# First token group of an mLSTM cell with a SwiGLU block: output gates loaded ahead of the weights, later loads in another order and other buffers, some gate work moved to VectorE

## The chip, the cores and the metric

The kernel runs on one core of one Trainium2 chip. The metric is the device time of one execution in microseconds. A core has a matrix engine (TensorE, PE in the profile; its weight loads are PEld), a vector engine (VectorE, DVE), a scalar engine (ScalarE, ACT), a general engine (GpSimd, POOL) and a sync engine (SyncE, SP), which here only issues transfers. Each engine works through its own instructions in order. Transfers between the main memory and the on-chip memory are issued from SP's queue and from ACT's queue (SPq and ACTq in the profile) and are carried out by 16 DMA engines. An instruction of ACT that stands behind a transfer's issue in ACT's program waits until that issue is through.

## The reference

Two stages follow each other. The first is a recurrent cell over 4 batches, 8 heads, 768 positions and 40 features (cut to what matters):

```python
for t in range(S):
    m_new = maximum(f_gate[t] + m, i_gate[t])
    C = exp(f_gate[t] + m - m_new) * C + exp(i_gate[t] - m_new) * outer(v[t], k[t])
    n = exp(f_gate[t] + m - m_new) * n + exp(i_gate[t] - m_new) * k[t]
    y[t] = sigmoid(o_gate[t]) * (C @ q[t]) / maximum(abs(n @ q[t]), 1)
```

The second is a feed-forward block over the 3072 tokens, with x the cell's output of 320 features per token: `(silu(x @ w_gate) * (x @ w_val)) @ w_out`, with 1536 hidden features. The cell's inputs are float32. The three weight matrices arrive as float64: 7.9 MB for the gate and value weights together and 3.9 MB for the output weights.

## The kernel before

**Groups.** The 768 positions are cut into 6 groups of 128. In each group the cell is computed in its parallel form: a matrix of weights per head made of running sums and running maxima of the gates, multiplied with the products of queries and keys, plus the contribution of the state carried over from earlier groups. Then 512 tokens (4 batches times 128 positions) go through the feed-forward block. The first group is special: its gates are handled by `first_*` functions, and while its feed-forward block runs, the weights are still being loaded and converted. Groups 2 to 6 use `gated` (L886) and `project_seven` (L794) with weights that are already in place; nothing in them is touched by the change.

**Weights.** `piece_load(p)` (L165) loads piece p of the weights as raw 64-bit words. Pieces 0 and 1 are one 128-column block of the gate and value weights each, pieces 2 to 6 are two blocks each, pieces 7 to 9 are the output weights. A piece of gate and value weights comes as three transfers: the gate half (64 partitions) on SP's queue, and the value half in two parts (the other 64 partitions) on ACT's queue. A piece of two blocks has 640 KB of gate weights and 512 KB plus 128 KB of value weights. The raw words land in a rotating buffer `raw` of two places, or in a "home", a stretch of a tile that is not used yet (`h_sb`, `wo_sb`).

**Conversion.** Block j becomes float32 in three steps: `scale(j)` (L216) on ACT (two instructions, L221 and L223), `join(j)` (L226) on DVE (L230 and L231), and `rounded(j)` (L235) on POOL or DVE (L238). The tile `top` between the first two steps has one buffer, so `scale` of the next block waits for `join` of this one.

**The first feed-forward block.** `hidden(0, m)` (L737) for m = 0 to 11 does ten matmuls on PE (20 records in the trace, L745) with block m, then the conversions that the table `ahead` names for m, then the SiLU on ACT (L750) and the product on DVE (L751). There are two pairs of result banks, so the matmuls of m wait for the product of m - 2; the banks are shared with the state of the first group, which ACT copies out at L142 (`first_kept`). After each m the functions in `slots[m]` follow. They prepare the second group: running sums of the later gates (`late_sums`, L315), their running maxima (`late_maxima`, L320), which are stored to main memory as `M_dram` (L1002 of `slots[1]`) and read back spread over the partitions into `w_sb` (`weights_load`, L501), the decay factors (`late_decay`, L325; an exponential on ACT in `slots[2]`; `decay_rows`, L719; `decay`, L727), transposes on PE that need that exponential (`late_turns`, L712), and transposes of keys and queries (`turn`, L343). `weights_sub` (L506), `weights_mask` (L510) and `weights_exp` (L531) make the second group's weights of `w_sb`. For the later groups a table `cap` (L516) and `weights_cap` (L523) do the masking instead.

**Order.** Each engine runs its instructions in the order in which the program names them; nothing reorders them. A further rule comes from how the program is built: eight semaphores tell of landings, they are dealt to the transfers in turn, and the issue of a transfer waits until the previous transfer with the same semaphore has landed. That earlier transfer can belong to the other queue. The built program names each such wait.

Of the kernel before, what the change touches and what calls it, by code (L numbers as in the profile page):

```python
# [13 lines left out]
AF = mybir.ActivationFunctionType  # L14
# [5 lines left out]
SUB = 64  # L20
# [4 lines left out]
def kernel(  # L25
# [139 lines left out]
    def piece_load(p, home=None, parts=(0, 1, 2)):  # L165
        kind, m, n = PIECES[p]
        if kind == "gv":
# [4 lines left out]
            queues = (nc.sync,) + 2 * (nc.scalar,)  # L172
# [12 lines left out]
        if p < 2 and not homes:  # L185
            for x in (1, 0):
                homes[x] = conv.tile([128, 4 * NKC * 128], U32, name="raw")
        if p in homes:
            raw = homes[p]
        elif home is None:  # L190
            raw = conv.tile([128, 4 * NKC * 128], U32, name="raw")
        else:
            raw = home.rearrange("p a t -> p (a t)").bitcast(U32)
# [121 lines left out]
    def late_sums():  # L315
        nc.vector.tensor_tensor_scan(flat(f_sb), flat(keep1), flat(f_sb), 0.0, op0=ALU.mult, op1=ALU.add)
        nc.gpsimd.memset(step1, 0.0)
        nc.gpsimd.tensor_sub(i_sb, i_sb, f_sb)
# [191 lines left out]
    def weights_mask(P):  # L510
        for i in range(2):
            w = w_sb[half(i), heads(P)]
            nc.gpsimd.affine_select(w, w, compare_op=ALU.is_ge, fill=NEG, base=0, pattern=[[0, UH], [1, SUB]],
                                    channel_multiplier=-1)

# [137 lines left out]
    piece_load(0)  # L653
# [19 lines left out]
    first_scores(1)  # L673
    scale(0)
    piece_load(1)
    sig(0)
    fill("y", 4, True)
    first_own(2)
    first_x(2)
    first_gate(0, (G, G), G)  # L680
    fill("y", 3, True)
    first_own(3)
    fill("y", 6, False)
    sig(1)
    piece_load(2, h_sb[:, 1:1 + NKC], (0, 1))
    late_gates()
    first_x(3)
    seam(0, 0, (A, A, A, A))
    first_gate(1, (V, V), A)
    ps0 = first_state(0, "gen")  # L690
# [5 lines left out]
    piece_load(2, parts=(2,))  # L696
    scale(1)
    piece_load(3)
# [6 lines left out]
    late_sums()  # L705
# [292 lines left out]
    def load_all(dst, a, n):  # L998
# [9 lines left out]
    ahead.update({4: [6], 5: [7, 8], 6: [9], 7: [10], 8: [11], 9: [], 10: [], 11: []})  # L1008
    slots = {
        0: [run(load_all, k_sb, k, 1), run(piece_load, 4, wo_sb), run(load_all, q_sb, q, 1)],  # L1010
        1: [run(late_maxima), run(nc.sync.dma_start, out=M_dram, in_=flat(M_sb)), run(late_decay)],
        2: [run(piece_load, 5, h_sb[:, NH - NKC:]), run(nc.scalar.activation, step1, step1, AF.Exp), run(decay_rows)],
        3: [run(late_turns)],
        4: [run(piece_load, 6), run(decay), run(cap_table), run(weights_load, 1), run(load_all, v_sb, v, 1)],
        5: [run(turn, 0, (A, A), (A, V))],
        6: [run(turn, 1, (A, A), (A, V)), run(piece_load, 7)],
# [129 lines left out]
```

## Time and profile before

| what | us |
|---|---|
| median of 3 runs | 522.8 (519.88 to 525.58) |
| the profiled execution | 526.02 |
| its span, first to last instruction | 524.2 |
| PE busy in the span | 506.9 (97%) |
| DVE, POOL, ACT busy | 334.6, 259.1, 206.8 |

The profile is of one execution. Times in it count from the start of the span. The busy shares are means over stages with different limits: PE is the bound from about 60 us to the end, while the first 60 us, where the weights arrive, have waits. So the first stage has to be read by itself: in the chain of waits (the work that ended last, followed back), in the timelines of single engines, where a bracket gives the idle time before a row and what ended it, and in tables by stretch of time, whose last three columns are the granted clock of PE, the busy share of the DMA engines and the rate that they moved.

### The profile page before, as it was taken

To read this page: it belongs to the slowest core of one execution; us is meant where nothing else is said; L and a number is where in the kernel's file an instruction comes from. 1 tells how busy PE (TensorE), PEld (TensorE's weight loads), DVE (VectorE), ACT (ScalarE), POOL (GpSimd) and SP (SyncE) were. 2 spreads that over 40 slices of the span, in tenths; PEclk is the share of its full clock that TensorE was granted. 3 is DMA by queue.
4 is the path that set the end of the run, shared out by engine and by line. 5 is a ranking of instruction groups with operands and counts; after the bars stand their busy time and mean duration, and the time that the engine had idled before them with its cause. 6 is when DMAs were issued, how large, how long until landed. Compare 5 with 4: busy or idle time off the path is not lost.

```text
span 524.2 us, 15080 instructions
## 1 busy us (share of the span) xinstructions
PE 506.9 (97%) x6446; PEld 425.6 (81%) x6446; DVE 334.6 (64%) x541; ACT 206.8 (39%) x400; POOL 259.1 (49%) x278
## 2 busy tenths in 40 slices
PE   9988499999999999999999999999999999999997
PEld 3843254676788999988899998899988899988897
DVE  5759358688878858867656867656847655233421
ACT  3552555447652227623137523137522231133210
POOL 3304134746777782455761455761455760166720
PEclk9999699999999999999999999999999999999999
DMA  9999998689830897230996230797100200100001
GB/s 144 186 202 142 188 193 234 96 171 124 143 38 3 128 136 84 56 38 6 139 132 74 54 39 5 136 130 78 41 1 10 43 5 14 39 1 0 1 14 39
DMA packets 205499, 43.31 MB, mean 83 GB/s; under 512 B 193432, under 2 KB 200600, under 8 KB 205432
## 3 DMA queue, kind: packets, MB, share of 16 engines
q1 hardware_dynamic: 202836, 38.34, 47.6%
q10 hardware_dynamic: 2596, 4.00, 4.0%
q8 instruction: 51, 0.84, 0.7%
q14 instruction: 16, 0.13, 0.1%
HBM read 35.68 MB, written 4.01 MB: 76 GB/s over the span
## 4 chain that ended last, share of the span: by engine, by line
PE 89%; DMA 6%; SPq 4%; issue 1%; ACT 0%; ACTq 0%; DVE 0%; DVEq 0%
PE gv_x L893 25%; PE o_ps L816 22%; PE gv_y L893 20%; PE gv_ps L745 8%; PE o_ps L762 5%; DMA o_sb<-in_o_gate_dram 2%; PE inter L422 2%; PE sp L373 2%; PE intra L431 2%; SPq L196 2%; DMA h_sb<-in_moe_w_val_dram 2%; DMA q_sb<-in_q_dram 2%; PE add L399 1%; SPq L248 1%; SPq L138 1%
## 5 line engine op out<-in xcount | busy, mean ns | idle before, releaser
L893 PE MATMUL gv_x<-xT,wgv_sb 64*128 64x256 f32 x720 | 89.7, 377 | 0.0
L893 PEld LDWEIGHTS gv_x<-xT,wgv_sb 64*128 64x128 f32 x720 | 70.0, 187 | 7.9 <-issue 0.2
L816 PE MATMUL o_ps<-wo_sb,h_sb 128*128 128x160 f32 x480 | 67.4, 300 | 0.0
L816 PEld LDWEIGHTS o_ps<-wo_sb,h_sb 128*128 128x128 f32 x480 | 65.6, 190 | 1.7 <-issue 1.7
L745 PE MATMUL gv_ps<-xT,wgv_sb 64*128 64x512 f32 x240 | 59.0, 625 | 2.6 <-ACT top L221 1.2
L941 ACT ACTIVATE h_sb<-gv_x 128x256 f32<-128x256 f32 x30 | 11.5, 384 | 118.0 <-PE gv_x L893 118.0
L745 PEld LDWEIGHTS gv_ps<-xT,wgv_sb 64*128 64x128 f32 x240 | 24.9, 196 | 30.8 <-issue 24.7
L893 PE MATMUL gv_y<-xT,wgv_sb 64*128 64x256 f32 x360 | 44.2, 376 | 0.0
L893 PE MATMUL gv_y<-q_sb,wgv_sb 64*128 64x256 f32 x360 | 44.2, 376 | 0.0
L893 PEld LDWEIGHTS gv_y<-q_sb,wgv_sb 64*128 64x128 f32 x360 | 35.2, 187 | 3.9
L893 PEld LDWEIGHTS gv_y<-xT,wgv_sb 64*128 64x128 f32 x360 | 35.2, 187 | 3.9
L384 POOL TENSOR_TENSOR vw_sb<-v_sb,w_sb 128x656 f32<-128x656 f32 x10 | 14.9, 1490 | 40.7 <-ACT w_sb L529 40.6
L816 PE MATMUL o_ps<-wT,S 128*128 128x160 f32 x240 | 33.4, 299 | 0.0
L816 PEld LDWEIGHTS o_ps<-wT,S 128*128 128x128 f32 x240 | 32.9, 190 | 0.0
L893 PE MATMUL gv_x<-q_sb,sw 64*128 64x256 f32 x240 | 31.2, 376 | 0.0
L529 ACT ACTIVATE w_sb<-w_sb,g_T 128x64 f32<-128x64 f32 x128 | 31.0, 333 | 0.0
L914 POOL TENSOR_TENSOR h_sb<-tmp 128x512 f32<-128x512 f32 x13 | 16.5, 1269 | 24.0 <-ACT tmp L913 24.0
L914 POOL TENSOR_TENSOR h_sb<-x_sb 128x512 f32<-128x512 f32 x12 | 15.8, 1313 | 24.6 <-ACT x_sb L913 24.6
L893 PE MATMUL gv_y<-q_sb,sw 64*128 64x256 f32 x200 | 27.5, 389 | 0.3 <-issue 0.3
L934 POOL TENSOR_TENSOR tmp<-tmp 128x512 f32<-128x512 f32 x15 | 20.0, 1330 | 15.7 <-DVE tmp L933 15.7
L783 POOL TENSOR_TENSOR S<-h_sb 128x256 f32<-128x256 f32 x30 | 22.6, 753 | 9.2 <-DVE h_sb L914 7.3
L933 DVE TENSOR_TENSOR tmp<-tmp,gv_y 128x1024 f32<-128x1024 f32 x15 | 18.1, 1205 | 14.2 <-PE gv_y L893 12.5
(228 smaller groups left out, 993.2 us busy)
## 6 DMA issues: line engine op xcount, KB each, us to landing
w_sb<-M_dram SPq DMA_DIRECT2D x10, 512.0 KB, 7.0
v_sb<-in_v_dram SPq DMA_DIRECT2D x12, 320.0 KB, 5.9
o_sb<-in_o_gate_dram SPq DMA_DIRECT2D x12, 320.0 KB, 4.4
raw<-in_moe_w_out_dram SPq DMA_DIRECT2D x3, 1280.0 KB, 6.2
k_sb<-in_k_dram SPq DMA_DIRECT2D x10, 320.0 KB, 7.5
x_sq<-k_sb SPq DMA_DIRECT2D x64, 40.0 KB, 2.0
q_sb<-in_q_dram SPq DMA_DIRECT2D x32, 64.0 KB, 3.2
out_dram<-tmp SPq DMA_DIRECT2D x24, 80.0 KB, 1.7
```

The source lines that it names most:

```text
L196: queue.dma_start(out=raw[r].rearrange("p (a d) -> p a d", a=a)[:, cs], in_=w.bitcast(U32))
L384: eng.tensor_tensor(vw_sb[:, heads(P)], v_sb[:, heads(P)], w_sb[:, heads(P), last].to_broadcast([128, UH, D1]), op=ALU.mult)
L529: nc.scalar.activation(w_sb[:, h], w_sb[:, h], AF.Exp, bias=g_T[:, n, h:h + 1], scale=-1.0)
L745: nc.tensor.matmul(ps[i], lhsT=wgv_sb[half(i), m, kc, :], rhs=x[half(i), kc, :], start=(kc == 0), stop=(kc == NKC - 1))
L762: nc.tensor.matmul(ps[u], lhsT=hid(g, m)[:, ts(u, L)], rhs=wo_sb[:, m, :], start=(m == 0), stop=(m == NFC - 1))
L783: eng.tensor_tensor(S1[:, k], lo[:, second_half], hi[:, second_half], op=ALU.add)
L816: nc.tensor.matmul(node[x][:, i], lhsT=lhs(k)[:, ts(i, L)], rhs=rhs(k), start=start and k == 0 and i == 0, stop=stop and k == KH - 1, skip ...
L893: nc.tensor.matmul(ps[:, i, cols], lhsT=lhs(c)[half(i)], rhs=rhs(c)[half(i)], start=start and c == 0, stop=stop and c == n - 1, skip_group ...
L914: (nc.vector if k == KH - 1 else nc.gpsimd).tensor_tensor(h_sb[:, 2 * k + 1], uw[:, 0], uw[:, 1], op=ALU.mult)
L933: nc.vector.tensor_tensor(uw, uw, y, op=ALU.add)
L934: nc.gpsimd.tensor_tensor(uw[:, :, second_half], uw[:, :, second_half], uw[:, :, first_half], op=ALU.add)
L941: nc.scalar.activation(h[:, first_half], x[:, 0, first_half], AF.Silu)
```

## The change

- In the first group the output gates (`o_sb`) are loaded directly behind q, k and v; piece 0 follows them and piece 1 comes at once after piece 0. The value halves of both are issued from ACT after the copies of the first group's transposes. Both sigmoids (`sig`) stand ahead of the second set of scores, and `scale(0)` after the first gating.
- Piece 2 is loaded in one call. Piece 3 goes into the end of `h_sb`, piece 4 into the buffer that piece 1 leaves (`homes[4] = homes[1]`), piece 5 into `wo_sb`, piece 6 into `raw`. Piece 4 is now called before the second group's keys.
- From piece 5 on, all three transfers of a piece are on SP's queue.
- `late_sums` moves into `slots[1]`, `late_maxima` and the store of `M_dram` into `slots[2]`, `late_decay` and its exponential into `slots[3]`, `decay_rows`, `late_turns` and the cap table into `slots[4]`, `decay` into `slots[7]`. `weights_load`, pieces 5 and 6 and the values of the second group follow the store of `M_dram` in `slots[2]`, all on SP.
- The subtraction in `late_sums` is on VectorE. The mask of the second group is a maximum with the cap table on VectorE (`weights_cap`, in `slots[6]`) instead of four selections on GpSimd.
- `ahead` converts one block in each of m = 5 to 9 instead of two in m = 5 and one in m = 6 to 8.

```diff
--- before.py
+++ after.py
@@ -169,7 +169,7 @@
             gate_w, val_w = (w[:, m * 128:(m + n) * 128].rearrange("(c p) f -> p c f", p=HP) for w in (moe_w_gate, moe_w_val))
             src = [(slice(0, HP), slice(0, NKC), gate_w), (slice(HP, 128), slice(0, NKC - 1), val_w[:, 1:]),
                    (slice(HP, 128), slice(NKC - 1, NKC), val_w[:, 0:1])]
-            queues = (nc.sync,) + 2 * (nc.scalar,)
+            queues = (nc.sync,) + 2 * (nc.scalar if p < 5 else nc.sync,)
         else:
             a, d = n, DM
             src = [(slice(0, 128), slice(0, n), moe_w_out[m * 128:(m + n) * 128].rearrange("(a p) d -> p a d", p=128))]
@@ -183,8 +183,9 @@
                         nc.sync.dma_start(out=wgv_sb[r, m + x, cs], in_=w[:, :, ts(x, 128)])
             return
         if p < 2 and not homes:
-            for x in (1, 0):
+            for x in (0, 1):
                 homes[x] = conv.tile([128, 4 * NKC * 128], U32, name="raw")
+            homes[4] = homes[1]
         if p in homes:
             raw = homes[p]
         elif home is None:
@@ -315,7 +316,7 @@
     def late_sums():
         nc.vector.tensor_tensor_scan(flat(f_sb), flat(keep1), flat(f_sb), 0.0, op0=ALU.mult, op1=ALU.add)
         nc.gpsimd.memset(step1, 0.0)
-        nc.gpsimd.tensor_sub(i_sb, i_sb, f_sb)
+        nc.vector.tensor_sub(i_sb, i_sb, f_sb)
 
     def late_maxima():
         nc.vector.tensor_copy(step1[:, 0:1, 0:1], f0[0:BH, end].unsqueeze(1))
@@ -507,12 +508,6 @@
         gb = g_T[:, n, heads(P)].unsqueeze(2).to_broadcast([128, UH, SUB])
         nc.vector.tensor_tensor(w_sb[:, heads(P)], gb, w_sb[:, heads(P)], op=ALU.subtract)
 
-    def weights_mask(P):
-        for i in range(2):
-            w = w_sb[half(i), heads(P)]
-            nc.gpsimd.affine_select(w, w, compare_op=ALU.is_ge, fill=NEG, base=0, pattern=[[0, UH], [1, SUB]],
-                                    channel_multiplier=-1)
-
     def cap_table():
         nc.gpsimd.memset(cap, -3e38)
         for i in range(2):
@@ -650,7 +645,6 @@
     for x in range(B):
         first_inputs(1, x)
     turn_one(0, k_sb, kT, (V, A))
-    piece_load(0)
     load(o_sb, o_gate, 0, 0)
     load(o_sb, o_gate, 0, 1)
     for x in range(B):
@@ -670,39 +664,40 @@
     first_own(1)
     first_x(0)
     first_x(1)
-    first_scores(1)
-    scale(0)
+    piece_load(0)
     piece_load(1)
     sig(0)
+    sig(1)
+    first_scores(1)
     fill("y", 4, True)
     first_own(2)
+    piece_load(2, h_sb[:, 1:1 + NKC])
+    late_gates()
     first_x(2)
     first_gate(0, (G, G), G)
+    scale(0)
     fill("y", 3, True)
     first_own(3)
+    first_x(3)
     fill("y", 6, False)
-    sig(1)
-    piece_load(2, h_sb[:, 1:1 + NKC], (0, 1))
-    late_gates()
-    first_x(3)
     seam(0, 0, (A, A, A, A))
     first_gate(1, (V, V), A)
+    piece_load(3, h_sb[:, NH - NKC:], (0,))
     ps0 = first_state(0, "gen")
     ps1 = first_state(1, "gen")
     join(0)
     rounded(0, V)
     seam(0, 1, (A, V, V, A))
     fill("add", 14, False)
-    piece_load(2, parts=(2,))
+    piece_load(3, parts=(1, 2))
     scale(1)
-    piece_load(3)
+    piece_load(4)
     first_kept(0, ps0, V)
     join(1)
     first_kept(1, ps1, A)
     rounded(1, V)
     nc.scalar.activation(warm, warm, AF.Silu)
     convert(2, V)
-    late_sums()
 
 
     pair = early.tile([BH, PP], F32)
@@ -1005,16 +1000,17 @@
     on_vector = (9, 10, 11)
     ahead = {m: [m + 2] for m in range(4)}
     ahead[0] = []
-    ahead.update({4: [6], 5: [7, 8], 6: [9], 7: [10], 8: [11], 9: [], 10: [], 11: []})
+    ahead.update({4: [6], 5: [7], 6: [8], 7: [9], 8: [10], 9: [11], 10: [], 11: []})
     slots = {
-        0: [run(load_all, k_sb, k, 1), run(piece_load, 4, wo_sb), run(load_all, q_sb, q, 1)],
-        1: [run(late_maxima), run(nc.sync.dma_start, out=M_dram, in_=flat(M_sb)), run(late_decay)],
-        2: [run(piece_load, 5, h_sb[:, NH - NKC:]), run(nc.scalar.activation, step1, step1, AF.Exp), run(decay_rows)],
-        3: [run(late_turns)],
-        4: [run(piece_load, 6), run(decay), run(cap_table), run(weights_load, 1), run(load_all, v_sb, v, 1)],
+        0: [run(load_all, k_sb, k, 1), run(load_all, q_sb, q, 1)],
+        1: [run(late_sums)],
+        2: [run(late_maxima), run(nc.sync.dma_start, out=M_dram, in_=flat(M_sb)), run(weights_load, 1),
+            run(piece_load, 5, wo_sb), run(piece_load, 6), run(load_all, v_sb, v, 1)],
+        3: [run(late_decay), run(nc.scalar.activation, step1, step1, AF.Exp)],
+        4: [run(decay_rows), run(late_turns), run(cap_table)],
         5: [run(turn, 0, (A, A), (A, V))],
-        6: [run(turn, 1, (A, A), (A, V)), run(piece_load, 7)],
-        7: [run(weights_sub, 1, 0), run(weights_mask, 0), run(weights_sub, 1, 1), run(weights_mask, 1), run(nc.gpsimd.memset, q_sb, 0.0)],
+        6: [run(turn, 1, (A, A), (A, V)), run(weights_cap, 0), run(weights_cap, 1), run(piece_load, 7)],
+        7: [run(nc.gpsimd.memset, q_sb, 0.0), run(decay), run(weights_sub, 1, 0), run(weights_sub, 1, 1)],
         8: [run(weights_exp, 0), run(weights_exp, 1), run(weigh_values, G, 0), run(weigh_values, G, 1),
             run(piece_load, 8)],
         9: [run(do_scores), run(do_weigh, 0), run(do_weigh, 1), run(do_decayed, 2), run(load_all, o_sb, o_gate, 1)],
```

## The prediction

> **What bounds the kernel now.** I read the page's slices first, to see where PE isn't full.
>
> ```profile
> span 524.2 us, 15080 instructions
> ...
> PE   9988499999999999999999999999999999999997
> ...
> PEclk9999699999999999999999999999999999999999
> DMA  9999998689830897230996230797100200100001
> ```
>
> A slice is 13.1 us. PE is full everywhere but in the first five slices; slice 5 (52 to 66 us) is at 4 tenths with a granted clock of 6 tenths. The DMA engines are full through the first seven. So the loads rule the first stage, and PE the rest. PE's timeline of that stage:
>
> ```profile
> 36.00 5.72 PE L745 MATMUL gv_ps<-xT,wgv_sb 64*128 64x512 f32 x20 [0.47 <-ACT C L142]
> 42.50 8.85 PE L745 MATMUL gv_ps<-xT,wgv_sb 64*128 64x512 f32 x38 [0.78 <-DVE h_sb L751]
> 51.28 0.49 PE L716 MATMUL tp_g<-ident,i_sb 32*128 32x32 f32 x5
> 59.52 0.74 PE L716 MATMUL tp_g<-ident,keep 32*128 32x32 f32 x5 [7.75 <-ACT keep L1002]
> 60.18 7.58 PE L745 MATMUL gv_ps<-xT,wgv_sb 64*128 64x512 f32 x20
> ...
> 78.88 13.10 PE L745 MATMUL gv_ps<-xT,wgv_sb 64*128 64x512 f32 x60
> ```
>
> One wait stands out: 7.75 us before the transposes of late_turns, for ACT's exponential of `keep` (L1002). The 20 matmuls of m = 4 behind it took 7.58 us; the last row has 60 in 13.10 us, 4.37 us per m. The granted clock tells why:
>
> ```profile
> 51.80:59.50 7.70, 0.00 (x0) 0.00 (x0) 0.59 (x2) 2.05 (x3) 0.51 (x1) 0.78 1.37 155
> 59.50:61.00 1.50, 1.48 (x7) 1.11 (x9) 1.08 (x3) 1.48 (x3) 0.00 (x0) 0.50 1.05 230
> 65.50:67.70 2.20, 2.20 (x11) 0.70 (x7) 0.00 (x0) 0.00 (x0) 1.94 (x4) 0.82 1.11 193
> ```
>
> A mean of 0.78 over 7.7 us idle at full or half clock means that the clock was halved 4.3 us into the idle time (0.22 x 2 x 7.7 = 3.4 us of half clock), and the last row puts its return near 66.3. Price: 7.58 - 4.49 = 3.1 us beside the 7.75. Why the exponential is late stands in ACT's and DVE's rows and in the chain of waits:
>
> ```profile
> 46.78 1.54 DVE L323 TENSOR_TENSOR_SCAN M_sb<-keep,M,i_sb 32x640 f32<-32x640 f32 x1
> ...
> 48.55 0.81 DVE L328 TENSOR_TENSOR keep<-m_in,M_sb 32x640 f32<-32x640 f32 x1
> ```
> ```profile
> 46.43 0.58 ACT L750 ACTIVATE tmp<-gv_ps 128x512 f32<-128x512 f32 x1
> 54.84 2.56 ACTq L196 DMA_DIRECT2D h_sb<-in_moe_w_val_dram  x2
> 57.44 1.28 ACT L1002 ACT_TABLE_LOAD   x1 [10.42 <-DMA q_sb<-in_q_dram]
> ```
> ```profile
> 40.98 7.59 SPq L196
> 48.57 0.05 issue
> 48.62 8.25 DMA q_sb<-in_q_dram
> 56.87 0.02 issue
> 56.89 0.51 ACTq L196
> ...
> 58.73 0.74 ACT keep L1002
> ```
>
> The maxima M_sb were ready at 48.32, the exponential's input at 49.36. ACT stood from 47.0 to 54.84 and to 56.89 at two issues of piece 5's value half, which reuse the semaphores of two transfers of the other queue (the built program names them: the gate half into wo_sb, and the first half of q_sb, landed 56.87).
>
> **The change part by part.**
>
> *The stall goes.* No transfer is issued on ACT behind piece 4's value half, and that is issued before the copy of the state. The exponential then waits for its data alone: DVE has two more instructions ahead of it (the scan of late_sums, and the subtraction in place of POOL's), but nobody waits for a foreign landing. So 7.75 + 3.1 = 10.85 us are to be had, if nothing else is late.
>
> *The start (costed at nothing).* Gates ahead of weights let sig, first_gate and the last copies of xT come earlier; ACT's wait in the middle of m = 1 (0.47 us, row 36.00) was for the same copy of the state, behind an issue that waits for piece 2. In the new order that copy stands behind piece 4's issues, which wait for two parts of piece 2. The same bytes must arrive before it (q, k, v, gates, pieces 0 to 2), so m = 1 goes on at 35 to 37, as before. What is won or lost here, at most the 1.2 us of the first gap and some 2 us at this one, is covered by the next wait, below.
>
> *From m = 1 to m = 7.* Without waits: 36.5 + 4.1 (rest of m = 1) + 0.2 + 3 x 4.5 (m = 2 to 4) + 1.0 (late_turns) + 4.5 + 1.0 (turn, 32 transposes) + 4.5 + 1.0 + 4.5 = 70.8. So PE wants block 8, the first of piece 5, at 71; before, m = 8 began at 78.88 + 4.37 = 83.25.
>
> *Piece 5 is the new limit.* It stands on SP behind the store of M_dram and behind weights_load, which waits for that store to land. Before, the issues were:
>
> ```profile
> 53.87 2.16 SPq L1002 DMA_DIRECT2D M_dram<-M_sb  x1
> 62.56 5.76 SPq L504 DMA_DIRECT2D w_sb<-M_dram  x2
> ```
>
> So M_dram landed at 62.5. Ahead of it stand the same transfers before and after: pieces 0 to 3, one more piece, keys and queries of group 2. The rates by stretch:
>
> ```profile
> 4.00:14.00 10.00, 9.95 (x100) 4.80 (x99) 4.71 (x13) 4.24 (x9) 2.52 (x5) 1.00 1.34 178
> ...
> 46.00:50.00 4.00, 4.00 (x20) 2.34 (x19) 3.84 (x7) 1.01 (x2) 0.66 (x1) 1.00 0.64 62
> 50.00:52.00 2.00, 1.77 (x12) 0.74 (x9) 1.97 (x5) 0.00 (x0) 1.23 (x1) 1.00 0.86 224
> ...
> 66.00:70.00 4.00, 4.00 (x20) 1.58 (x18) 0.92 (x2) 1.25 (x2) 1.44 (x4) 0.96 1.21 199
> ```
>
> From 46 to 50 the queues ran nearly empty: 62 GB/s instead of 178, 4 x 116/178 = 2.6 us lost, at SP's issue that the chain shows from 40.98 to 48.57. In the new order small and large loads don't alternate there. And ACT's value half of 54.84 no longer shares the time before the store (0.3 MB, 1.7 us). M_dram then lands at 62.5 - 2.6 - 1.7 = 58.2. w_sb is 1.05 MB at 199 GB/s, 5.3 us, and 1.5 us from issue to first bytes: 65.0. Piece 5, 1.31 MB, follows without a gap at the 224 GB/s of a gate half alone: 5.9 us, and 1 us to land: 71.9. As bounds: at 178 GB/s it lands at 73.4; if M_dram were only held by its data (M_sb, before at 48.32, moves behind one more product and the 0.8 us subtraction, to about 50) and landed at 54, piece 5 would land at 67.7. I take 71.9, nearest to the rows of this stretch.
>
> From landing to ready, a block went like this before:
>
> ```profile
> 69.35 0.79 ACT L221 ACTIVATE top<-wo_sb 128x640 f32<-128x640 f32 x1 [0.96 <-DVE dec L731]
> ```
> ```profile
> 70.17 0.50 DVE L230 TENSOR_SCALAR wgv_sb<-top 128x640 uint32<-128x640 uint32 x1 [0.82 <-ACT top L221]
> 70.70 0.82 DVE L231 SCALAR_TENSOR_TENSOR wgv_sb<-top,wgv_sb 128x640 uint32<-128x640 uint32 x1
> ```
> ```profile
> 71.70 1.56 POOL L238 TENSOR_TENSOR wgv_sb<-wgv_sb,low 128x640 int32<-128x640 int32 x1 [4.14 <-DVE wgv_sb L231]
> ```
>
> 3.9 us from 69.35 to 73.26. So m = 8 begins at 71.9 + 0.1 + 3.9 = 75.9 instead of 83.25: **7.3 us earlier**, with a new wait of some 5 us on PE, broken only by the half microsecond of `decay`. Behind ACT's waiting scale(8) queue the SiLU of m = 6 and the copies of turn; PE needs the SiLU for m = 8's banks and the copies for the banks of `decay`, so they add nothing.
>
> *Mask and sums on VectorE (costed at nothing).*
>
> ```profile
> 84.66 2.35 DVE L508 TENSOR_TENSOR w_sb<-g_T,w_sb 128x1024 f32<-128x1024 f32 x2
> ```
> ```profile
> 85.96 6.76 POOL L513 TENSOR_SCALAR_AFFINE_SELECT w_sb<-w_sb 64x1024 f32<-64x1024 f32 x4 [9.79 <-DVE w_sb L508]
> ```
> ```profile
> 78.60:91.70 13.10, 13.10 (x76) 5.93 (x70) 10.90 (x12) 7.81 (x12) 5.57 (x4) 1.00 0.81 233
> ```
>
> Two maxima of the shape of L508 add about 2.35 us to DVE, which is 10.9 of 13.1 us full there (last row, a stretch); POOL loses 6.76 us. The subtraction has the shape of L328, about 0.8 us. The cover is PE's own 4.4 us per m against some 3.5 us of DVE; if it failed, m = 9 or 10 would wait up to 2.4 us.
>
> *After m = 8* the later loads have slack: piece 6 lands 5.9 us behind piece 5, at 77.8, and its block 10 is wanted after two more m and the scores, at 87; group 2's values (0.66 MB at 178 GB/s, 3.7 us) land at 81.5, the first output weights (1.31 MB) by 87.4, wanted behind m = 11. What is won at m = 8 then stays, as PE hardly waits later; its waits from 105 us to the end were
>
> ```profile
> PE intra L431 <- issue: 0.5, 1, 0.5
> PE gv_y L893 <- issue: 0.3, 1, 0.3
> ```
>
> Sum: 526.0 - 7.3 = 518.7 on the profiled execution, which lies 3.2 above the median of the three runs; on the median, 522.8 - 7.3 = **515.5**.
>
> [...]
>
> **The rivals.**
> 1. *The loads come in time.* Piece 5 lands by 67.7, m = 8 begins at 71.7: 11.5 us won, 511. For it: M_sb is ready at 50. Against it: the store stands behind 1.3 MB of keys and queries on one queue.
> 2. *The change doesn't do it:* ACT is held at another landing ahead of the exponential, 522.8. Against it: the built program names none after piece 4.
> 3. *The new wait halves the clock:* PE idle for 3.9 us until `decay` and 5 in all, against 4.3 us in the rows. Then the same 3.1 us are paid again, and 4.2 stay: 518.6.
> 4. *Slower: one queue in series.* All of pieces 5 and 6, the spread w_sb and the values stand behind the store, which waits for M_sb; any delay of M_sb beyond the queries' issue (54 us, row 53.87) moves them one for one. With the clock's 3.1 us, break-even is m = 8 at 80.2, a landing at 76.2, that is M_dram at 62.5 instead of 58.2, as late as before. It costs 1% (5.2 us) when M_dram lands at 68: 528. Against it: M_sb has 4 us of slack.
>
> **How the numbers follow.** Forecast (515.5; own range 513 to 518) 0.42, hidden loads 0.15, halved clock 0.27, slower 0.10, no effect 0.06. One per cent, 5.2 us, is about what a measurement of this kernel can tell from no change; faster by that means below 517.6: 0.85 x 0.42 + 0.15 + 0.25 x 0.27 = 0.57; slower 0.10; the rest 0.33. The range goes from below the hidden case, 510, to the halved clock with piece 5 at its late bound (+1.5) and one more delay of 2 to 3 us, 523.
>
> **What would show it.** Right: no idle of PE before the transposes of `keep`; m = 5 starting near 56 instead of 68; the one long wait of PE before m = 8, ended by POOL L238 with ACT's wait for piece 5 (`wo_sb`) behind it; M_dram landed near 58; ACT issuing nothing behind piece 4. Wrong: a wait over 3 us anywhere else (m = 1 above all, if ACT stands at piece 4's issues), half clock behind m = 8, or w_sb late enough to hold the maxima on DVE.

## The result, and the profile after

The changed kernel takes 520.09 us (median of 22 executions, 517.19 to 522.72) against 522.87 us before (22 executions, 519.88 to 525.82): a ratio of 0.9946, 95% interval 0.9927 to 0.9966. It is faster by 2.8 us (by the interval 1.8 to 3.8). The forecast was 7.3 us. The two profiled executions differ by more than the medians: 526.02 us before, 518.82 us after.

The slices of the page of the kernel after (each 12.9 us; tenths of busy time, and of the granted clock):

```profile
span 516.9 us, 15071 instructions
...
PE   8999979999999999999999999999999999999997
...
PEclk9999989999999999999999999999999999999999
```

The slice that stood at 4 tenths before is full. What is left, apart from the first slice and the last, is one slice at 7 with a clock of 8 tenths, from 65 to 78 us. PE's timeline of the kernel after in that stage:

```profile
29.49 23.61 PE L740 MATMUL gv_ps<-xT,wgv_sb 64*128 64x512 f32 x100 [0.18 <-ACT xT L142]
...
54.32 0.49 PE L711 MATMUL tp_g<-ident,keep 32*128 32x32 f32 x5 [0.79 <-ACT keep L997]
...
71.89 0.53 PE L724 MATMUL dec_ps<-dec_r,halves 32*128 32x160 f32 x2 [1.92 <-ACT kT L142]
73.35 10.29 PE L740 MATMUL gv_ps<-xT,wgv_sb 64*128 64x512 f32 x40 [0.92 <-POOL wgv_sb L239]
...
103.22 0.79 PE L432 MATMUL intra<-v_sb,w_sb 64*64 64x41 f32 x38 [0.35 <-issue]
```

The stall of 7.75 us before the transposes of `keep` is a wait of 0.79. Blocks 0 to 4 run almost through. A new wait of 1.92 + 0.92 us stands before block 8, and the 40 matmuls of blocks 8 and 9 take 10.29 us, where 40 at full clock take 8.85 (a row of a later experiment). ACT's and DVE's timelines and the chain of waits of the kernel after say what the new wait is for:

```profile
69.44 0.79 ACT L222 ACTIVATE top<-wo_sb 128x640 f32<-128x640 f32 x1 [8.05 <-DMA wo_sb<-in_moe_w_val_dram]
...
71.28 1.04 ACT L142 COPY kT<-tp_kq 128x512 f32<-128x512 f32 x2
```
```profile
70.78 0.82 DVE L232 SCALAR_TENSOR_TENSOR wgv_sb<-top,wgv_sb 128x640 uint32<-128x640 uint32 x1
```
```profile
49.65 4.46 DMA M_dram<-M_sb
...
54.17 0.59 SPq L505
...
59.82 11.87 DMA raw<-in_moe_w_gate_dram
...
71.78 1.52 POOL wgv_sb L239
73.30 0.04 issue
73.35 10.29 PE gv_ps L740 x40
```

It is piece 5 (its home is `wo_sb`), behind the store of M_dram on SP, as the prediction had it: `scale(8)` waits 8.05 us for it, the copies of `kT` that PE's first wait names stand behind that in ACT's program, and the join on DVE and POOL's rounding follow. The chain's row at 59.82 is not piece 5 but the gate half of piece 6 (`raw`); it landed at 71.69, a tenth behind the end of that join (71.60), and the profile names what came last. In the second trace of this kernel the chain goes through piece 5's value half, from 59.67 to 69.40. The clock, in stretches of 2 us of the kernel after (third column from the end):

```profile
72.00:74.00 2.00, 1.08 (x4) 0.69 (x6) 2.00 (x3) 2.00 (x4) 2.00 (x2) 0.72 1.28 164
74.00:76.00 2.00, 2.00 (x6) 0.68 (x4) 1.97 (x4) 0.67 (x2) 1.04 (x1) 0.50 0.73 88
76.00:78.00 2.00, 2.00 (x12) 0.97 (x10) 1.86 (x3) 1.14 (x2) 0.00 (x0) 0.93 1.25 200
```

Clock lost: 2 x (0.28 + 0.50 + 0.07) = 1.70 us, that is 3.4 us at half clock.

Block 8 begins at 73.35 instead of 83.23, 9.9 us earlier, and the span ends 7.3 us earlier. So 2.6 us are given back behind the start of block 8, in this pair. The experiments ask two things: does each part of the mechanism hold, and where does the gain go?

### The profile page after: what moved, and what is told of

It reads as the page before. It is cut to its first block, busy times and chain, and to the rows that moved or that the text cites. A ratio compares the mean times of both kernels' runs of the same rounds, so it can differ in the third digit from the quotient of the medians.

```text
span 516.9 us, 15071 instructions
## 1 busy us (share of the span) xinstructions
PE 504.9 (98%) x6446; PEld 425.7 (82%) x6446; DVE 333.7 (65%) x544; ACT 206.5 (40%) x400; POOL 250.9 (49%) x273
## 4 chain that ended last, share of the span: by engine, by line
PE 85%; DMA 6%; DVE 4%; ACT 1%; SPq 1%; issue 1%; ACTq 1%; POOL 1%; DVEq 0%; POOLq 0%
PE gv_x L888 24%; PE o_ps L811 22%; PE gv_y L888 20%; PE o_ps L757 5%; PE gv_ps L740 4%; DMA raw<-in_moe_w_gate_dram 2%; PE inter L423 2%; PE sp L374 2%; DMA h_sb<-in_moe_w_gate_dram 2%; PE intra L432 2%; PE add L400 1%; DMA M_dram<-M_sb 1%; DMA i<-in_i_gate_dram 1%; DVE C L416 1%; SPq L197 1%
## 5 line engine op out<-in xcount | busy, mean ns | idle before, releaser
L740 PE MATMUL gv_ps<-xT,wgv_sb 64*128 64x512 f32 x240 | 56.8, 610 | 1.2 <-POOL wgv_sb L239 0.9
L740 PEld LDWEIGHTS gv_ps<-xT,wgv_sb 64*128 64x128 f32 x240 | 26.0, 192 | 26.1 <-issue 19.6
L239 POOL TENSOR_TENSOR wgv_sb<-wgv_sb,low 128x640 int32<-128x640 int32 x6 | 9.3, 1545 | 38.0 <-DVE wgv_sb L232 26.5
```

Source lines behind the costliest of these rows:

```text
L740: nc.tensor.matmul(ps[i], lhsT=wgv_sb[half(i), m, kc, :], rhs=x[half(i), kc, :], start=(kc == 0), stop=(kc == NKC - 1))
```

## The experiments

All ratios are against the kernel before, run beside the experiment.

| kernel | median us | ratio, 95% interval |
|---|---|---|
| before again | 523.82 | 1.0013, 0.9994 to 1.0032 |
| after again | 521.15 | 0.9962, 0.9945 to 0.9978 |
| before, value halves from piece 5 on SP | 517.20 | 0.9886, 0.9863 to 0.9909 |
| after, value halves on ACT | 523.83 | 0.9999, 0.9979 to 1.0019 |
| after, piece 5 ahead of the store | 516.97 | 0.9879, 0.9857 to 0.9901 |
| after, PE kept busy in the new wait | 520.88 | 0.9934, 0.9908 to 0.9960 |
| before, PE kept busy in the stall | 523.14 | 0.9982, 0.9961 to 1.0004 |
| after, piece 9 later | 519.57 | 0.9902, 0.9877 to 0.9928 |
| piece 5 ahead of the store, piece 9 later | 517.63 | 0.9881, 0.9849 to 0.9912 |
| the same, half of a later load left out | 515.34 | 0.9849, 0.9821 to 0.9877 |
| after, half of that load left out | 519.99 | 0.9928, 0.9903 to 0.9952 |
| before, half of that load left out | 524.14 | 1.0004, 0.9979 to 1.0030 |
| after, mask on GpSimd | 523.23 | 0.9989, 0.9968 to 1.0010 |

**Both kernels again, unchanged.** A blank line is added, so line numbers are higher by one.

> The kernel before, unchanged, for a second profile and for the granted clock of each execution. The forecast was a gain of 7.3 us, worked out on a profiled execution of 526.02 us; the medians differ by 2.8. Theory 1 (the profiled execution was one of the slow ones of a spread): the executions spread from 520 to 526 with a granted clock from about 0.997 down to 0.990, slower where the clock is lower, and a second profile shows a shorter wait of PE before the transposes of keep than 7.75 us, or little or no half clock behind it; median 522 to 523. Theory 2 (the wait and its half clock are always there, and the new kernel gives the gain back at a place that its profile doesn't show): all executions have a clock near 0.990, and a second profile has 7 to 8 us of wait and 3 us of half clock again.

> The changed kernel, unchanged, for a second profile. Theory 1: executions from 517 to 523 us, median 520, again slower where the clock is lower; the second profile has the wait before m = 8 again, 2 to 6 us in all, as piece 5 lands between 68 and 73 us. Theory 2: the second profile shows m = 8 near 73 us again and a wait somewhere behind m = 9 that the first one hadn't.

The medians differ by 2.7 us again. PE's timeline of the kernel before, second trace:

```profile
59.19 0.74 PE L717 MATMUL tp_g<-ident,keep 32*128 32x32 f32 x5 [8.14 <-ACT keep L1003]
59.85 6.91 PE L746 MATMUL gv_ps<-xT,wgv_sb 64*128 64x512 f32 x20
...
77.88 13.09 PE L746 MATMUL gv_ps<-xT,wgv_sb 64*128 64x512 f32 x60
```

The stall is there again, with the half clock behind it. Block 8 begins a third into the last row, at 82.23. In the kernel after the new wait is 1.77 + 0.91 us and blocks 8 and 9 take 10.40.

**The queue alone, and the change without it.**

```diff
 b_val_sp: before
-            queues = (nc.sync,) + 2 * (nc.scalar,)
+            queues = (nc.sync,) + 2 * (nc.scalar if p < 5 else nc.sync,)
 a_val_act: after
-            queues = (nc.sync,) + 2 * (nc.scalar if p < 5 else nc.sync,)
+            queues = (nc.sync,) + 2 * (nc.scalar,)
```

> The kernel before with one line of the change: the value halves from piece 5 on are issued on SP's queue. If ACT was held at those two issues alone, the exponential runs at about 50 us, the wait of PE before the transposes of keep (7.75 us) is gone, and the next limit is piece 5: on SP behind the store of M_dram, it lands near 63 to 65 us, block 8 is wanted for m = 8 near 70, so no wait over 1 us is left on PE: 4 to 9 us faster than before, 514 to 519. If the exponential was late for another reason (the table load, the data), the wait stays and the time is that of before, 522 to 524.

> The kernel after, but the value halves of piece 5 and 6 are issued on ScalarE again, as in the kernel before: the queue line of the change is undone, all its moves stay. Theory A (the queue alone removed the stall): ScalarE is held at these issues again, behind it keep, the turn and TensorE stand for about 6 to 8 us near 53 us, and the time goes back to that of the kernel before (523 to 525). Theory B (the new order and the new homes removed it): no wait over 2 us at the turn, and the time agrees with the kernel after within 1 us. Between: a shorter wait of 2 to 5 us.

PE's timeline of the kernel before with this one line:

```profile
52.60 0.47 PE L716 MATMUL tp_g<-ident,keep 32*128 32x32 f32 x5
53.01 4.56 PE L745 MATMUL gv_ps<-xT,wgv_sb 64*128 64x512 f32 x20
...
68.69 13.09 PE L745 MATMUL gv_ps<-xT,wgv_sb 64*128 64x512 f32 x60
```

And ACT's and PE's of the kernel after without it:

```profile
46.42 6.83 ACTq L197 DMA_DIRECT2D raw<-in_moe_w_val_dram  x2
...
58.16 0.73 ACT L997 ACTIVATE keep<-keep 32x640 f32<-32x640 f32 x1 [1.57 <-DVE keep L329]
```
```profile
58.95 0.74 PE L711 MATMUL tp_g<-ident,keep 32*128 32x32 f32 x5 [5.28 <-ACT keep L997]
```

The line decides on the stall. With it alone no wait stands before these transposes, block 8 begins at 73.0, and the kernel is 1.1% faster than before. (Its profiled execution, 519.04 us, is the highest of its six, with 3.4 us of clock lost, from 42 to 46 and from 102 to 108 us.) Without it ACT stands 6.8 us at two issues, the stall is back at 5.28 us, and nothing is won by the rest. There the delay takes one more step: the row at 58.16 waits for DVE's `keep`, and DVE had waited 4.39 us, to 54.16, for the `scale` that stood behind the two issues. The second issue went through just behind a landing of the other queue in both traces: `q_sb` at 56.87 before, `k_sb` at 52.74 here. So the cause named in the prediction, issues held on ACT, is shown; and the rest of the change, put on top of this line, makes the kernel slower: 517.2 against 520.1 to 521.2.

**Piece 5 ahead of the store.**

```diff
-        2: [run(late_maxima), run(nc.sync.dma_start, out=M_dram, in_=flat(M_sb)), run(weights_load, 1),
-            run(piece_load, 5, wo_sb), run(piece_load, 6), run(load_all, v_sb, v, 1)],
+        2: [run(piece_load, 5, wo_sb), run(late_maxima), run(nc.sync.dma_start, out=M_dram, in_=flat(M_sb)),
+            run(weights_load, 1), run(piece_load, 6), run(load_all, v_sb, v, 1)],
```

> The changed kernel with piece 5 issued ahead of the store of M_dram. If piece 5's place behind the store and the spread w_sb is the new limit, piece 5 lands 8 to 10 us earlier, near 60, the wait before m = 8 (2.8 us in the profile of the changed kernel, and half clock for 3 us behind it) goes and nothing takes its place: 3 to 5 us faster than the changed kernel, 515 to 517. w_sb then lands 6 us later, near 68; if that counts (the maxima on VectorE wait for it), the wait moves to m = 9 and the time stays near 520.

PE's timeline:

```profile
70.30 0.53 PE L724 MATMUL dec_ps<-dec_r,halves 32*128 32x160 f32 x2
70.76 8.85 PE L740 MATMUL gv_ps<-xT,wgv_sb 64*128 64x512 f32 x40
```

The new wait and its half clock are gone, and 4.2 us are won on the kernel after (516.97 against 521.15; the intervals of the ratios lie apart). That is 2.8 us of wait and about 1.5 of clock. So the place of piece 5 behind the store is what the rest of the change costs. This version beats both kernels; it doesn't beat the one line alone (517.20), so no gain of the rest is shown.

**The half clock by itself.** TensorE multiplies constants in the waits (`burn`), so that it isn't idle there.

```diff
 b_warm: before
-        3: [run(late_turns)],
+        3: [run(burn, 32), run(late_turns)],
 a_warm: after
-        7: [run(nc.gpsimd.memset, q_sb, 0.0), run(decay), ...
+        7: [run(nc.gpsimd.memset, q_sb, 0.0), run(burn, 10), run(decay), ...
```

> The kernel before, with 32 matrix products on constants on TensorE's queue ahead of the turning of the late gates, so that TensorE works through most of the stall of 7.75 to 8.1 us but the stall stays as long as it was. My prediction put 3.1 us of its 10.85 on the half clock behind the stall. If that term is right and nothing gives it back, the kernel ends 2.4 to 3.1 us ahead of the kernel before and block 4's 20 products take 4.6 us instead of 6.9. Rival: what is won there is given back further on, as in the kernel after, and the gain is below 1.5 us. Second rival: the stall grows with the added work, since TensorE is late for the turn, and nothing is won (within 0.5 us).

> The kernel after, with ten matrix products on constants put on TensorE's queue ahead of the decay of block m = 8, so that TensorE works through most of the new wait of about 1.9 us. Nothing else is changed. Theory A (the half clock behind the new wait is a loss of its own): block 8's 40 products take about 8.8 us instead of 10.3 to 10.4, the wait that is left (on the conversion of piece 5) stays near 0.9, and the kernel ends 1.0 to 1.6 us ahead of the kernel after. Theory B (the half clock is hidden by a later wait of the same length, so that it costs nothing): block 8 is shorter all the same, a wait between 85 and 145 us grows by as much, and the time agrees with the kernel after within 0.4 us. The filled wait itself must not come back in either.

PE's timeline of the kernel before with the products:

```profile
59.38 4.56 PE L745 MATMUL gv_ps<-xT,wgv_sb 64*128 64x512 f32 x20
...
74.96 0.27 PE L338 MATMUL tp_kq<-ident,k_sb 64*128 64x64 f32 x1 [0.72 <-ACT kT L142]
```

No half clock: 4.56 us instead of 6.91 or 7.58. But the median is only 1.0 us lower, and the interval reaches to no change. At the end of this block PE is 2.8 us ahead of the second trace of before (63.9 against 66.8), at 77 us only 0.8: waits at the transposes of k, the longest of which the row shows, take it back. So the 3.1 us of my sum were mostly hidden behind another wait. The kernel after with the products tells little: they stand in the bank that `kT` frees, so they waited 1.76 us themselves and then pushed block 8 to 74.84. Blocks 8 and 9 took 8.85 us, and their end came where it was. Its median doesn't differ from the kernel after by more than the intervals.

**The wait inside `intra`.** Behind block 8, PE waits up to 1.7 us in the middle of a run of matmuls that needs nothing new. Piece 9 moves ahead of it and in it: from 102 to 104 us its queue took 102.5% of the DMA engines' time (a row below). Piece 9 is issued one block later in two kernels:

```diff
-        11: [run(do_inter, 1, 0), run(do_gather, 1, 0, False), run(piece_load, 9),
+        11: [run(do_inter, 1, 0), run(do_gather, 1, 0, False),
...
-        0: [run(do_attend, 1, 1), run(convert, 14), ...
+        0: [run(do_attend, 1, 1), run(piece_load, 9), run(convert, 14), ...
```

> The kernel after with piece 5 issued ahead of the store of the maxima (as in the experiment before, 516.97 us) and piece 9, the 1.3 MB of output weights whose packets are small, issued one block later, behind m = 11 rather than in it. Theory A (TensorE's waits of 0.5 to 1.4 us at the products named intra near 100 us, ended by nothing that the profile names, are instruction fetches that stand behind piece 9 on the DMA engines): these waits go below 0.5 us in all, and the kernel ends 1.0 to 1.5 us ahead of 516.97. Theory B (these waits have another cause): intra waits 1.5 to 2 us as before, the time stays within 0.5 us of 516.97, or above where piece 9 comes too late for its conversion.

> The kernel after with piece 9, the 1.3 MB of output weights issued in m = 11, issued one block later; piece 5 stays where the change put it. Theory A (TensorE's waits at intra near 104 us are its own instruction fetches standing behind piece 9, and the half clock behind such a wait is part of the loss): the waits of 0.4 to 1.8 us inside intra go, no half clock follows between 104 and 112 us, and the median comes 1 to 2.5 us ahead of the kernel after (518 to 519.5). Theory B (what is won there is given back by the later stream of transfers or by piece 9's own conversion): the waits go, but the median agrees with the kernel after within 0.7 us.

PE's timeline of an execution of the kernel after with a long wait, and the DMA queues of its stretch from 102 to 104 us (packets, MB, share of the engines):

```profile
103.23 0.64 PE L433 MATMUL intra<-v_sb,w_sb 64*64 64x41 f32 x26
105.48 1.14 PE L433 MATMUL intra<-v_sb,w_sb 64*64 64x41 f32 x38 [1.61 <-issue]
106.55 10.14 PE L758 MATMUL o_ps<-wo_sb,h_sb 128*128 128x320 f32 x32
```
```profile
q1 hardware_dynamic: 814, 0.71, 102.5%
q8 instruction: 1, 0.02, 3.2%
```

The same place in the kernel after with piece 9 later:

```profile
104.34 1.12 PE L432 MATMUL intra<-v_sb,w_sb 64*64 64x41 f32 x64
105.39 8.88 PE L757 MATMUL o_ps<-wo_sb,h_sb 128*128 128x320 f32 x32
```

The 64 matmuls run through, and the 32 behind them take 8.88 us instead of 10.14, so the half clock behind the wait goes too. The median is 0.5 and 1.6 us below the two of the kernel after; by the ratios to the kernel before, which ran beside each, it is 2.3 and 3.1 us, and the intervals touch in the first case and lie apart in the second. In the version with piece 5 ahead of the store the wait goes as well, but its time stays, 517.63: there a wait of 1.34 us and half clock came up at 151 us. In the traces of the kernel after, of its other versions and of the one line alone, with piece 9 in its old place, this wait is there in nine of ten (0.35 to 1.74 us; one execution of the kernel after has none); with piece 9 later it is there in none of three. So it is shown for these versions that the load's place causes the wait. Five traces of the kernel before and its other versions have no such wait, with piece 9 in the same slot. That the wait is for an instruction fetch is only my reading of the row, with one packet of 0.02 MB on the queue called instruction; no run shows it.

**The later loads.** The prediction gave them slack. SP's timeline before, behind block 8:

```profile
85.87 5.07 SPq L138 DMA_DIRECT2D o_sb<-in_o_gate_dram  x2
94.60 4.71 SPq L357 DMA_DIRECT2D q_sb<-in_q_dram  x8
...
102.20 8.18 SPq L357 DMA_DIRECT2D q_sb<-in_q_dram  x8
111.78 2.07 SPq L504 DMA_DIRECT2D w_sb<-M_dram  x2
```

And after:

```profile
85.18 6.39 SPq L138 DMA_DIRECT2D o_sb<-in_o_gate_dram  x2
91.62 5.90 SPq L358 DMA_DIRECT2D q_sb<-in_q_dram  x8
...
98.15 9.08 SPq L358 DMA_DIRECT2D q_sb<-in_q_dram  x8
107.40 2.06 SPq L505 DMA_DIRECT2D w_sb<-M_dram  x2
```

Before, SP stood idle from 90.9 to 94.6 and from 110.4 to 111.8, waiting for buffers that the computation frees. These are two of the five idle times of 1.1 to 3.7 us between its rows up to 145 us. After, none over 0.3 us is left between the rows from 85 to 145 us: most of the slack is used up, and VectorE waits for loads, 3.5 to 6.2 us in all between 100 and 160 us in the four traces of the kernel after, and not once in the three of before. Nor does it in the trace with the one line alone, where block 8 comes as early (73.0) and SP still has idle times of 0.6 to 2.9 us. So the late loads come with the change's order of loads, not with an early block 8 as such. Half of one load is left out in three kernels, so that a part of the third group's scores isn't computed:

```diff
-            load_squares(live["k_sq"], k, 2)
+            load_squares(live["k_sq"], k, 2, (0,))
```

> The kernel after, with half of one later load left out: of the 16 small transfers that bring the third group's k in squares, 8 are not issued (half of the heads keep zeros there, so a part of the third group's scores is not computed; nothing else changes). In the trace of the kernel after SP issues its transfers without a gap over 0.2 us from 54 to 145 us, and the fourth group's k, the last of them, lands at 147.8 to 148.9 us, just ahead of the transposition on VectorE that waits for it; in the kernel before SP stood idle five times for 1 to 4 us in the same stretch. Theory A (this stream of transfers is the limit that takes back the gain between 105 and 145 us): the last load lands about 5 us earlier, the waits on gv_y and sp near 141 to 145 us go, and the kernel ends 0.6 to 1.5 us ahead of the kernel after; no more, because the rest was lost ahead of 105 us. Theory B (the stream has slack, as my prediction said of the later loads): the time agrees with the kernel after within 0.4 us.

> The same half of a load left out of the version with piece 5 ahead of the store and piece 9 one block later (517.63 us), where VectorE waited 1.73 us for the fourth group's k (landed 146.33), TensorE 1.34 us behind it, and half a clock followed. Theory A (the stream of transfers is the limit): the fourth group's k lands near 141, all three go, and the kernel ends 1.5 to 3 us earlier, at 514.5 to 516. Theory B: the time stays within 0.5 us of 517.63 and the waits near 150 us are there with another releaser.

> The same half of a load left out of the kernel before. There SP waited for buffers between its transfers, so the stream was not the limit. Theory A: the time agrees with the kernel before within 0.5 us, and TensorE shows the same waits. Theory B' (the stream is the limit in both kernels, whatever the change does ahead of it): it ends as much earlier as the kernel after does with the same load cut, 1 us or more.

DVE's timeline of the version with piece 9 later, with the whole load:

```profile
146.51 2.37 DVE L364 STREAM_TRANSPOSE kT<-x_sq 128x1024 f32<-128x1024 f32 x2 [1.73 <-DMA x_sq<-in_k_dram]
```

With half of it the median falls from 517.63 to 515.34 us, as expected by theory A, but the intervals overlap, and the profiled execution is the highest of six (518.44; the others 514.68 to 515.66). Its trace shows what theory A named: DVE waits for no k, the wait of 1.34 us at `intra` is 0.53, and no half clock follows. It also has a new wait: PE stands 1.87 us at 120.6 us for converted output weights, behind 4.7 us in which DVE waited for `w_sb`. The kernel before gains nothing (1.0004, the interval 1.1 us down to 1.6 us up). The kernel after comes out 0.1 to 1.2 us lower than in its own two measurements, with overlapping intervals, which decides nothing. So theory A is borne out by the waits on DVE, here and below; its size on the median is not firm.

**The mask back on GpSimd.** The four selections come back (`weights_mask`, behind `weights_sub`), and the maxima with the cap table go.

> The kernel after with the mask of the second group's gates on GpSimd again, as in the kernel before. My prediction costed the move of mask and sums to VectorE at nothing. If that holds, the time agrees with the kernel after within 0.5 us, block m = 8 starts within 0.5 us of 73.4 and the scores behind m = 9 at the same distance. Rival: the mask stands behind piece 5's conversion on GpSimd, w_sb is late for the exponentials of m = 8, and the sums of m = 9 to 10 wait 1 us or more: 1 to 2 us slower. Rival on the other side: VectorE, busy with capping at 66 to 75 us, delays kT and the conversions, and without it the new wait shortens by 0.5 to 1 us.

POOL's and PE's timelines:

```profile
78.04 6.76 POOL L514 TENSOR_SCALAR_AFFINE_SELECT w_sb<-w_sb 64x1024 f32<-64x1024 f32 x4 [4.59 <-DVE w_sb L509]
```
```profile
73.51 8.85 PE L746 MATMUL gv_ps<-xT,wgv_sb 64*128 64x512 f32 x40 [0.90 <-POOL wgv_sb L239]
...
92.04 0.31 PE L400 MATMUL add<-vw_sb,k_sb 64*64 64x41 f32 x2 [3.04 <-DVE w_sb L381]
```

The time is that of the kernel before. With the mask on POOL the sums of the second group wait 3.04 us, with 1.7 us of clock lost behind it from 92 to 96 us: more than the first rival of this experiment said. So the move of the mask was not only free: once block 8 comes 10 us earlier, it keeps 2 to 3 us of the gain. (The edit also puts `decay` ahead of the clearing of `q_sb` again; the subtraction in `late_sums` was not tried by itself.) And the row at 73.51 is a surprise: the same wait before block 8 (1.77 + 0.90 us), but no half clock behind it.

**More executions to read.** Both kernels unchanged, one execution each.

> The kernel after, unchanged, one more execution to read. Theory A (its executions differ by how much half clock falls behind two waits, the one ahead of m = 8 and the one at intra near 104 us): the time is 517 plus the time lost to half clock there (0 to 2.9 us in block 8's 40 products beyond 8.85 us, and 0 to 2.2 us in the output products behind intra), within 0.8 us. Theory B (they differ by the stall's remains or by the transfers behind 110 us): block 8 and the products behind intra take the same as in the profile after whatever the time.

> The same once more, with the same expectations: an execution near 522 shows both stretches at half clock, one near 519 only the first, one near 517 neither.

> The kernel before, unchanged, one more execution to read: its two traces so far, 526.02 and 524.46 us, differ by 1.6 us, and the difference is there by 66 us, in the stall (7.7 and 8.1 us) and the time before and behind it. Theory A (executions of before differ by when the gate row is ready, by the stall and by the half clock behind it, all ahead of 70 us): the difference to the profile of before is there by 70 us and does not change by more than 0.5 us behind it. Theory B: it comes behind 85 us, from the transfers.

521.59, 521.39 and 523.42 us. By theory A the first two should have come out at 517 + 1.70 + 1.26 = 520.0 and 517 + 1.55 = 518.6, within 0.8. They are 1.6 and 2.8 us above, so half clock at these two places isn't enough to tell the executions apart. The first shows both stretches of half clock, as said, and more waiting at intra; the second has a third place. DVE's and PE's timelines of the second:

```profile
134.89 2.37 DVE L365 STREAM_TRANSPOSE kT<-raw 128x1024 f32<-128x1024 f32 x2 [3.99 <-DMA o_sb<-in_o_gate_dram]
```
```profile
140.35 1.13 PE L889 MATMUL gv_x<-xT,wgv_sb 64*128 64x256 f32 x8 [2.04 <-DVE C L417]
```

DVE stands 3.99 us at the third group's keys (the profile names the gate's load that is issued right behind them), the state's sum queues behind that, and PE waits 2.04 us for it. That is the stream of loads late enough to hold PE. PE's timeline of the kernel before, third trace:

```profile
57.52 0.73 PE L717 MATMUL tp_g<-ident,keep 32*128 32x32 f32 x5 [4.09 <-ACT keep L1003]
58.18 7.11 PE L746 MATMUL gv_ps<-xT,wgv_sb 64*128 64x512 f32 x20
...
76.41 13.10 PE L746 MATMUL gv_ps<-xT,wgv_sb 64*128 64x512 f32 x60
```

Here the stall is 4.09 us, with 1.7 us of half clock already lost from 42 to 47 us. PE is 2.5 us ahead of the first trace at the start of block 8 and 2.4 at 290 us: executions of before differ ahead of block 8, as theory A said.

## Why the prediction was wrong in size

Each trace can be cut at the start of block 8 (for the kernel before a third into the row of 60 matmuls):

| trace | block 8 at | from there to the span's end |
|---|---|---|
| before, three traces | 83.2, 82.2, 80.8 | 441.0, 440.5, 440.8 |
| after, four traces | 73.4, 73.4, 73.8, 74.1 | 443.6, 444.8, 446.0, 445.4 |
| before, value halves on SP | 73.0 | 444.3 |
| after, piece 5 ahead of the store | 70.8 | 444.0 |

**The stall and its cause: right.** ACT at two issues whose semaphores belong to the other queue; the one line shows it both ways. Its length was read from one trace: 7.75 us there, 8.14 and 4.09 in two others.

**The half clock behind it, 3.1 us: mis-sized as a gain.** The block took 2.4 and 2.6 us too long in the two other traces. Taken away by itself, it is worth about 1 us on the median, with no change inside the interval, because waits at 75 us hide the rest.

**The start and m = 1 to 7, at nothing: right.** Rows 29.49 to 54.32 have waits of 0.2 and 0.8 us.

**Piece 5 as the new limit: right in kind, too late by 2.5 us.** The conversion began at 69.44 instead of 72.0 and block 8 at 73.35 instead of 75.9. M_dram landed at 54.1 and not 58.2: the chain's row gives the store 4.46 us from 49.65. I had carried over the slow transfers ahead of the old store and taken off only part of them; the store went out as soon as M_sb was ready (49.62). The stretch behind it was too short: from M_dram's landing to `scale(8)` it took 15.3 us and not 13.8. No run shows two terms of that stretch by themselves, the 1.5 us from an issue to its first bytes and the 1 us to land; the runs show only the 15.3 us in all. The wait that I put at 5 us was 1.92 + 0.92. The conversion itself, 3.9 us, came out as forecast.

**Mask and sums on VectorE, at nothing: right.** No row of PE behind block 8 in the kernel after waits for `w_sb`. And the move of the mask is needed, as the experiment shows.

**After m = 8 what is won stays: this step failed.** The traces of the table that reach block 8 at 74 us or earlier need 443.6 to 446.0 us from there, those of before 440.5 to 441.0: 2.6 to 5.5 us are given back. Three things take them. First, 1.4 to 1.7 us of half clock behind the new wait, in the four traces of after; I had held this as the third rival, at 3.1 us. Second, waits inside `intra` near 104 us of 0.35, 0.86 and 1.61 us in three of the four, in one with 1.7 us of half clock behind. Third, small waits from 140 to 157 us and, in one trace, the 2.04 us for loads that land late. Against the mean of before, 440.8, the four give back 2.8, 4.0, 5.2 and 4.6 us; the waits and half clock found, without the 0.5 us at `intra` that before has too, come to 2.4, 3.0, 4.9 and 4.2 of them. The waits inside `intra` are there without any new wait too (the table's last rows: 1.06 us with 1.7 of half clock behind, and 1.38), so they are the price of an early block 8 with piece 9 where it stands, not of the place of piece 5. I had checked the landings of pieces 6 and 7 and of the second group's values against their dates, and no load of the third and fourth groups; and I read "PE hardly waits later" in a trace where the stall had given every later load 10 us more.

**The carry to the median: wrong as well.** On the profiled pair 9.9 us at block 8 less 2.6 behind give 7.3 us, the very number forecast, by two misses that cancel. But that trace of before is its kernel's slowest of three, and that of after the fastest of four. The means of the traces are 82.1 + 440.8 and 73.7 + 445.0: 8.4 us earlier, 4.2 given back, 4.2 left; the medians of the many executions say 2.8. The rest, 1.4 us, I can't place: two of the three traces of before lie above the medians of their runs.

The rivals: hidden loads (511) fell to the row at 71.89; no effect (522.8) and slower (528) too. The third, 518.6, was nearest in mechanism and in time.

**The clock.** What falls at half clock differs between executions of one kernel, and between kernels with nearly the same wait. Before block 8 that wait was followed by 8.85 us for the 40 matmuls with the mask on GpSimd, by 10.29, 10.40, 10.55 and 10.40 in the four traces of the kernel after, and by 11.72 and 11.80 in two experiments (half of the later load left out, piece 9 later). In the three traces of before the clock fell 4.3, 3.3 and 3.1 us into the idle time ahead of the transposes of `keep`, and came back 6.8, 5.4 and 5.8 us after the work began (59.52 to 66.3, 59.19 to 64.6, 57.52 to 63.4). In one execution of the kernel after it fell near 105.7 us, behind a single wait of 1.61 us (the row at 105.48 above). So the 4.3 us against which my third rival set its 5 us of wait were an estimate from one trace, and the other runs don't bear it out; no run shows what sets the fall or the return.

## What to carry to other kernels

Before a gain at one point of the critical path is counted to the end, move every later consumer forward by that gain and ask whether its load would still be there; idle time between the issues of a transfer queue tells how much is left (here five times 1.1 to 3.7 us before, and none over 0.3 after). Change the smallest thing first: one line that took the value halves of two pieces off ACT's queue gave twice the gain of the whole change. And read two or three executions before a stall's length goes into a sum.

## What the runs showed of the hardware

- The clock lost, summed over the stretches of 2 us from 4 to 150 us, was 0 (piece 5 ahead of the store), 1.7 (three traces of after), 3.4 (the fourth) or 5.1 us (all three of before); at half clock that is 0, 3.4, 6.8 or 10.2 us.
- With the mask on GpSimd, a wait of 1.77 + 0.90 us, broken by 0.53 us of work, was followed by no half clock, and the 40 matmuls of blocks 8 and 9 took 8.85 us. With piece 9 later they took 11.80 us, 3.0 more, behind a wait of 1.86 + 0.90 us.
- PE stopped for 1.61 us (103.87 to 105.48, one execution of the kernel after) inside a run of 64 matmuls, with no releaser named in the profile; from 102 to 104 us the queue of the loads took 102.5% of the DMA engines' time. With piece 9 one block later the stop was gone in three traces of three.
- Two issues on ACT's queue stood for 6.83 us (46.42 to 53.25, the kernel after with its value halves on ACT), and ACT's next computation, behind them in its program, began at 53.35.
